# Two blocks' denominators per step, output pairs of a block side by side, and a new order of steps in a gated pair of linear-attention blocks

## The chip, the cores and the metric

One of the eight cores of a Trainium2 chip runs the whole kernel. The metric is the device time of one execution in microseconds (us); lower is better. All times below are in us unless marked ns.

## What is computed

The input x has 2048 tokens of 640 numbers in bf16. Two linear-attention blocks, A and B, read the same x with weights of their own; their outputs are mixed token by token with a gate. Cut to what matters:

```python
def block(x, wqkv, wo):                       # 32 heads of 20 columns
    q, k, v = (x @ wqkv) split in three, each [32, 2048, 20]
    phi = lambda t: where(t > 0, t + 1, exp(t)) + 1e-6
    pq, pk = phi(q), phi(k)
    kv  = einsum("sd,se->de", pk, v)          # per head
    z   = sum over tokens of pk
    num = pq @ kv
    den = pq . z + 1e-6
    return concat_heads(num / den) @ wo

g = sigmoid((x * gate_w).sum(-1))
out = g * block_A(x) + (1 - g) * block_B(x)
```

## The kernel before

The kernel is one core's program whose order is made when it is built. Every instruction is given to a small planner (`Sched`) with its engine, a cost and the buffers that it reads and writes. The planner goes through time by its own costs and fixes the order on each engine and the slot of each pooled buffer; semaphores are then set where one engine depends on another. TensorE alone is different: its steps run in the order written, and that order is the string `MAIN` (L47 to L54). Pools stand for space: `ps` are the 8 banks of PSUM, `eq` three pairs of buffers for exp(q), `po` saved partial sums of the output, `os` and `ot` staging for the output, `gt` and `sv` partial sums of the earlier stages.

The stages, in order of time:

- **K** (to 48 us): x @ Wk for 16 token tiles of 128 and both blocks (L618, L619), then phi on ScalarE and VectorE.
- **G** (`g_unit`, tokens `Gu.n`, L1000): instead of k^T v the kernel forms G = pk^T x for the ten groups of 128 columns of A and B, two groups per unit u = 0 to 4. Each unit is a 2x2 block product done with seven products and sums of operands (Strassen's scheme in Winograd's form), so n runs over 1, 2, 5, 6, 3, 7, 4; a product is eight matmuls of 320 columns, about 1.09 us. Results go through `GT` (L1034, L1105) and a transposing DMA into `GSA` and `GSB`. Extra columns give z, spread by heads into `DEN` (L1048).
- **Q** (`qu_unit`, tokens `Qg.n`, L887): q of the first 1024 tokens (blocks 0 and 1 of 512 tokens), five units of seven products with two or three matmuls of 512 columns. Sums are made on VectorE (`qcm`, L901), then exp and relu on ScalarE (L917, L918), a clip (`qt`, L926) and an add (`qs`, L928) on VectorE give pq.
- **R** (`qp_unit`, tokens `RgX`, L970): q of the other 1024 tokens (blocks 2 and 3) as plain products, ten matmuls of 512 columns into a pair of banks, then exp (L981), relu (L982), clip (L984) and add (L985), each on 1024 columns at once.
- **kvA, kvB** (L1146): kv = G^T Wv per block, masked to the heads on VectorE (`kvm`, L1124). **wA0 to wB1** (`wp_burst`, L1177): kv @ wo in halves, copied out by ScalarE (L1193), written to DRAM (`wpsA`, `wpsB`) and read back as `WP` with another layout. **T1**: four sums of WP's quarters (`t_mat`, L1323).
- **den b** (`den`, L1253): the denominators of block b. Twenty matmuls with 32 columns of weights each: four strips (A and B, two halves of the block) of 256 columns in one bank, five groups of heads summed. VectorE adds the epsilon and multiplies by the gate's factor (L1266; the factor 1 + exp(-+a) was spread by GpSimd at L823 and transposed by a DMA into `GTX`); ScalarE takes ln and exp(-ln) (L1276, L1277). Four DMAs then spread the result over the 128 partitions (`fx`; they read as XN<-PKS for even blocks and TX<-PKS for odd ones), and VectorE scales pq by it (`pqs`, L1309), in two halves for the blocks in `PQH`, block 0 alone.
- **S b** (`s_blk`, L1343): four sums of block b's scaled pq.
- **O** (`Pair`, tokens `Oi.n`, L1378): the output of 256 tokens (pair i = 0 to 7, two per block) as a 2x2 block product with seven products of five matmuls of 320 columns, 0.68 us each, of pq by WP or sums of both. Between them stand copies PSUM to PSUM (o1f, L1417), saves (o2s, o5s, L1394), evictions (o11, o21, L1422, L1443) on ScalarE and sums (o12, o22, L1401) on VectorE. The result is stored in rows of 128 tokens (`o_store`, L1360).

SP issues nearly all DMAs, in the planner's order; ScalarE's queue takes some of wpsB and one of the last stores. SP waits in order, so an issue whose data is late holds all later ones. What sets the order around the change are thus four things: `MAIN` for TensorE, the planner's order on VectorE and ScalarE (an instruction that waits holds all behind it), SP's order, and the bank pairs and `eq` slots that a step must take over from an earlier one.

Of the kernel before, what the change touches and what calls it, by code (L numbers as in the profile page):

```python
# [7 lines left out]
ALU = mybir.AluOpType  # L8
# [3 lines left out]
D = 640  # L12
# [34 lines left out]
MAIN = """G0.1 G1.1 G2.1 G0.2 G1.2 G2.2 G0.6 G0.5 G1.5 G1.6 G1.3 G0.7 G1.7 G0.3 G2.5 G0.4 G1.4 G2.6 Q0.1 G2.3  # L47
Q0.5 Q1.1 Q0.2 Q0.6 Q1.6 Q2.1 Q1.2 Q0.7 Q1.5 Q0.3 Q0.4 Q1.7 G2.7 G3.1 Q3.1 Q2.6 G2.4 Q1.4 Q2.2 Q3.6
Q3.2 G3.2 Q1.3 Q2.5 G4.1 Q3.5 Q2.7 G3.5 Q2.3 Q3.7 Q4.1 G3.6 Q2.4 G3.3 Q3.3 Q4.6 G3.7 Q4.5 Q4.7 Q3.4
G3.4 Q4.3 G4.6 Q4.4 G4.5 Q4.2 kvA G4.2 G4.7 wA0 G4.3 G4.4 wA1 LA den0 R0A kvB den1 wB0 R1A  # L50
S0 R1B R4A R0B wB1 R3A T1 O0.5 O1.5 R2A R3B R2B O0.1 S1 O1.1 R4B O0.2 O1.2 O0.6 O1.6
O1.3 O2.5 den2 O0.7 O3.1 O2.1 O0.3 O3.2 O2.2 O3.5 den3 S2 O0.4 O3.6 O3.3 O1.7 O4.1 O2.6 S3 O4.5
O3.7 O4.6 O2.3 O2.7 O4.2 O5.1 O4.7 O5.5 O5.2 O5.6 O1.4 O4.4 O3.4 O6.1 O6.5 O4.3 O5.7 O6.2 O7.1 O7.5
O2.4 O5.4 O6.6 O5.3 O6.3 O7.6 O7.2 O6.7 O7.7 O7.3 O6.4 O7.4"""  # L54
PB = {}
PQH = (0,)
# [41 lines left out]
class Sched:  # L98
# [97 lines left out]
    def pick(self, b, t, skip=()):  # L196
# [15 lines left out]
        c = [(max(have[i] for i in range(s, s + b.n)), s) for s in b.at if all(i in have for i in range(s, s + b.n))]  # L212
        return min(c) if c else None
# [82 lines left out]
def body(nc, A_x, A_wqkv, A_wo, B_x, B_wqkv, B_wo, gate_w, out, log=None):  # L296
# [79 lines left out]
    OST = {"os": [PKS[:, 8192 + D * k : 8832 + D * k] for k in range(NOS)], "ot": [PKS[:, SSB + D * k : SSB + D * k + D] for k in range(NOT)]}  # L376
# [3 lines left out]
    DNR = PKS[:, SSB + 12288 : SSB + 12800].bitcast(f32)  # L380
    FR = [PKS[:, SSB + 12800 + 256 * n : SSB + 13056 + 256 * n] for n in range(2)]
# [15 lines left out]
    POS = [EKT[:, 644 * k : 644 * k + 640] for k in range(4)] + [PKS[:, 12288 + 640 * k : 12928 + 640 * k] for k in range(5)]  # L397
    POS = [a.bitcast(f32) for a in POS]

# [31 lines left out]
    def dve1(n):  # L431
        return 155 + 1.04 * n
# [383 lines left out]
    dst = GGX.rearrange("p (b k s h) -> p k b s h", b=NB, k=2, s=4)  # L816
    for i, X in enumerate(XS):
        src = (GI if i else GE)[:, :].rearrange("p (b s k) -> p k b s", b=NB, k=2)
        for k in range(2):
            a = src[:, k].unsqueeze(3).to_broadcast([128, NB, 2, 32])  # L820
            op(
                "POOL",
                lambda e, d=dst[:, k, :, 2 * i : 2 * i + 2, :], a=a: e.tensor_scalar(d, a, 1.0, None, op0=ALU.add),  # L823
                600.0,
                ins=bge + [bgi],
                outs=[bx],
                name="ggx",
            )
# [412 lines left out]
    pqs_op, stt_op = {}, {}  # L1241
    bfx = {}

    fx_op = {}

    def den(b):
        ps, b1, b2 = Buf("dn", "ps"), Buf("dr"), Buf("ff")

        def fn(e):
            for g in range(NC):  # L1250
                for s in range(4):
                    i, h = s // 2, s % 2
                    r = e.matmul(  # L1253
                        PS[32 * s : 32 * s + 32, ps.slot, 0:256],
                        ZM[:, NC * i + g, :],
                        PQ[XS[i], b][:, g, 256 * h : 256 * h + 256],
# [5 lines left out]
        op("PE", fn, 850.0, ins=list(bz.values()) + [bpq[b, k] for k in range(2 * NC)], outs=[ps], name="den%d" % b)  # L1262
        ff, gt = FR[b % 2], GTX[:, 256 * b : 256 * b + 256]
        stt_op[b] = op(
            "DVE",
            lambda e: e.scalar_tensor_tensor(DNR, PS[:, ps.slot, 0:256], EPS, gt, op0=ALU.add, op1=ALU.mult),  # L1266
            dve1(256),
            ins=[ps, bgt],
            outs=[b1],
            after=list(stt_op.values()),  # L1270
            prio=-1,
            name="dg%d" % b,
        )

        b3 = Buf("ln")
        op("ACT", lambda e: e.activation(DNR, DNR, ACT.Ln), act_cost(256), ins=[b1], outs=[b3], prio=-1, name="ln%d" % b)  # L1276
        stt_op[b, 1] = op("ACT", lambda e: e.activation(ff, DNR, ACT.Exp, scale=-1.0), act_cost(256), ins=[b3], outs=[b2], after=fx_op.get(b - 2, []), prio=-1, name="rc%d" % b)  # L1277
        fx_op[b] = []
        for i, X in enumerate(XS):
            pqs_op[X, b] = []  # L1280
            hs = []
            for h in range(2):
                src = ff[64 * i + 32 * h : 64 * i + 32 * h + 32, :]
                bx = Buf("fx")
                hs.append(bx)
                fx = FX[X, b][:, 256 * h : 256 * h + 256]
                fx_op[b].append(
                    dma(
                        "SP",
                        "fx%s%d%d" % (X, b, h),  # L1290
                        fx,
                        bass.AP(tensor=src.tensor, offset=src.offset, ap=[src.ap[0], [0, 4], src.ap[1]]),
                        65536,
                        ins=[b2],
                        outs=[bx],
                        after=pqs_op.get((X, b - 2), []),
                        prio=-1,
                        issue=450.0,
                        rate=150.0,
                    )  # L1300
                )
            for lo, hi in ((0, 256), (256, 512)) if b in PQH else ((0, 512),):
                bs = Buf("pqs")
                for h in range(lo // 256, hi // 256):
                    bfx[X, b, h] = bs
# [224 lines left out]
```

## Time and profile before

| what | us |
|---|---|
| median of 3 runs (177.5 to 178.05) | 177.81 |
| the profiled execution | 177.45 |
| its span, first to last instruction | 176.0 |
| TensorE busy in it | 172.0 |
| VectorE busy | 123.6 |
| ScalarE busy | 120.2 |
| granted TensorE clock | 1.0 |

Where TensorE's time goes, by the chain that ended last (shares of the span): O steps 22%, G 21%, K 19% and 6%, R 12%, Q 11%, all others 1% or less each. Times of day in the profiled execution, counted from the span's start: the first G at 48, the first Q at 67.9, kvA at 101.5, den0 at 108.3, kvB at 111.3, the first O at 125.6, den2 at 141.1, den3 at 146.6, the last O ends near 173.8, the last copy at 174.4, and the last store lands at 176.0.

A row of the timeline gives the start, the duration, the engine, the line, the operation, what is written and read and how many; in square brackets how long the engine was idle before it and what ended that. ScalarE's and VectorE's instructions overlap a little when they stand back to back, so starts can be closer than durations. A row of a stretch gives its length, then the busy time of PE, PEld (weight loads), DVE (VectorE), ACT (ScalarE) and POOL (GpSimd), the granted clock, the busy time of the DMA engines and GB/s.

### The profile page before, as it was taken

How to read it: one execution, taken by the hardware profiler on the slowest of the kernel's cores; microseconds unless marked ns; L12 is line 12 of the kernel's file. 1: busy time of each engine (PE TensorE's matmuls, PEld its weight loads, DVE VectorE, ACT ScalarE, POOL GpSimd, SP SyncE). 2: the span in 40 equal slices, each digit the busy share in tenths (PEclk: the TensorE clock that was granted, in tenths of full speed). 3: DMA queues.
4: the chain of work that ended last, by engine and by line, in shares of the span. 5: the costliest groups of instructions: out<-in, count | busy, mean ns of one | idle time of the engine just before them, and what ended most of it. 6: DMA issues, size and time to landing. Idle time of an engine off the chain costs nothing.

```text
span 176.0 us, 3334 instructions
## 1 busy us (share of the span) xinstructions
PE 172.0 (98%) x1323; PEld 108.4 (62%) x1337; DVE 123.6 (70%) x212; ACT 120.2 (68%) x224; POOL 4.9 (3%) x16
## 2 busy tenths in 40 slices
PE   9999999999999999999999999899999999999995
PEld 5555555555577776566666666555555666777773
DVE  2275986999999449574659763469999936995222
ACT  5278888988831214999698938799989745436431
POOL 1000000000002500000000000000000000000000
DMA  7979999300000158982701532877522013413143
GB/s 196 296 142 191 185 375 366 123 2 0 4 0 0 32 101 215 155 124 51 182 0 37 148 79 49 214 158 242 160 49 79 0 56 82 130 47 111 38 149 112
DMA packets 33036, 20.59 MB, mean 117 GB/s; under 512 B 18261, under 2 KB 32893, under 8 KB 33021
## 3 DMA queue, kind: packets, MB, share of 16 engines
q1 hardware_dynamic: 32062, 19.76, 45.1%
q10 hardware_dynamic: 958, 0.63, 1.3%
q8 instruction: 10, 0.16, 0.4%
q14 instruction: 6, 0.04, 0.1%
HBM read 10.88 MB, written 4.26 MB: 86 GB/s over the span
## 4 chain that ended last, share of the span: by engine, by line
PE 96%; ACT 1%; issue 1%; DVE 1%
PE ps L1378 22%; PE ps L1000 21%; PE ps L618 19%; PE ps L970 12%; PE ps L887 11%; PE ps L619 6%; PE ps L547 1%; PE ps L1177 1%; PE ps L1253 1%; PE ps L560 1%; PE ps L1146 1%; ACT EQ L981 1%; ACT EQ L917 0%; DVE PKS L1124 0%; ACT PQ L918 0%
## 5 line engine op out<-in xcount | busy, mean ns | idle before, releaser
L618 PE MATMUL ps<-WKW,XT 128*128 128x512 bf16 x154 | 43.4, 383 | 0.0
L619 PE MATMUL ps<-WKW,XT 128*128 128x128 bf16 (+1 forms) x160 | 35.3, 221 | 0.3
L618 PEld LDWEIGHTS ps<-WKW,XT 128*128 128x128 bf16 x160 | 15.8, 99 | 19.1 <-DVE XT L577 0.3
L664 ACT ACTIVATE EKT<-ps 128x640 bf16<-128x640 f32 x32 | 22.3, 704 | 6.6 <-PE ps L619 5.9
L1000 PE MATMUL ps<-TX,PKS 128*128 128x321 bf16 (+1 forms) x160 | 24.2, 300 | 0.0
L1000 PEld LDWEIGHTS ps<-TX,PKS 128*128 128x128 bf16 x160 | 15.6, 98 | 7.5
L1000 PE MATMUL ps<-XN,PKS 128*128 128x321 bf16 (+1 forms) x120 | 18.0, 300 | 0.0
L619 PEld LDWEIGHTS ps<-WKW,XT 128*128 128x128 bf16 x160 | 15.8, 99 | 0.0
L1029 ACT ACTIVATE EKT<-ps 128x321 f32<-128x321 f32 (+1 forms) x15 | 6.4, 442 | 13.4 <-PE ps L1000 10.9
L1000 PEld LDWEIGHTS ps<-XN,PKS 128*128 128x128 bf16 x120 | 11.5, 98 | 5.3 <-issue 0.2
L744 DVE TENSOR_TENSOR PKS<-PKS 128x1280 bf16<-128x1280 bf16 (+2 forms) x20 | 13.6, 702 | 0.1
L667 DVE TENSOR_SCALAR EKT<-EKT 128x1280 bf16<-128x1280 bf16 (+1 forms) x18 | 8.1, 453 | 5.9 <-ACT EKT L664 5.7
L1034 DVE TENSOR_TENSOR WKW<-ps,EKT 128x320 bf16<-128x320 f32 x15 | 7.3, 489 | 6.9 <-PE ps L1000 6.8
L1401 DVE TENSOR_TENSOR PKS<-ps,PKS 128x320 bf16<-128x320 f32 x11 | 5.4, 489 | 9.0 <-PE ps L1378 8.8
L981 ACT ACTIVATE EQ<-ps 128x1024 bf16<-128x1024 f32 x10 | 10.2, 1022 | 2.0 <-PE ps L970 1.2
L970 PE MATMUL ps<-XT,WQA 128*128 128x512 bf16 x47 | 11.0, 379 | 0.5 <-issue 0.5
L970 PE MATMUL ps<-XT,WQB 128*128 128x512 bf16 x49 | 11.2, 379 | 0.1
L703 DVE SCALAR_TENSOR_TENSOR PKS<-ps,EKT 128x640 bf16<-128x640 f32 x12 | 9.8, 819 | 0.1
L917 ACT ACTIVATE EQ<-ps 128x512 bf16<-128x512 f32 x15 | 9.3, 617 | 1.0 <-DVE ps L901 0.5
L970 PEld LDWEIGHTS ps<-XT,WQB 128*128 128x128 bf16 x50 | 5.9, 117 | 4.8
L970 PEld LDWEIGHTS ps<-XT,WQA 128*128 128x128 bf16 x50 | 5.6, 119 | 4.8 <-issue 0.6
L676 ACT ACTIVATE PKS<-ps 128x640 bf16<-128x640 f32 x12 | 8.4, 698 | 0.0
(141 smaller groups left out, 301.5 us busy)
## 6 DMA issues: line engine op xcount, KB each, us to landing
out_dram<-PKS SPq DMA_DIRECT2D x15, 160.0 KB, 1.8
XN<-in_A_x_dram SPq DMA_DIRECT2D x1, 2240.0 KB, 9.4
WKW<-in_A_wqkv_dram SPq DMA_DIRECT2D x5, 160.0 KB, 3.6
WKW<-in_B_wqkv_dram SPq DMA_DIRECT2D x5, 160.0 KB, 4.0
WQA<-in_A_wqkv_dram SPq DMA_DIRECT2D x1, 800.0 KB, 11.0
WQB<-in_B_wqkv_dram SPq DMA_DIRECT2D x1, 800.0 KB, 13.7
WVA<-in_A_wqkv_dram SPq DMA_DIRECT2D x1, 800.0 KB, 5.0
PKS<-in_B_wqkv_dram SPq DMA_DIRECT2D x1, 800.0 KB, 5.0
```

The source lines that it names most:

```text
L618: e.matmul(a[:, 0:512], l, WK[X][:, c, 0:512], start=(c == 0), stop=(c == NC - 1))
L619: return e.matmul(a[:, 512:w], l, WK[X][:, c, 512:w], start=(c == 0), stop=(c == NC - 1))
L664: op("ACT", lambda e, i=i, ps=ps: e.activation(evg(i), psg(ps), ACT.Exp), act_cost(D), ins=[ps] + first, outs=[ek, b], name="ke")
L676: op("ACT", lambda e, X=X, ps=ps: e.activation(pkt(X, t), psg(ps), ACT.Relu), act_cost(D), ins=[ps], outs=[rk], name="kr")
L703: lambda e, X=X, i=i, ps=ps: e.scalar_tensor_tensor(pkt(X, t), psg(ps), 0.0, evg(i), op0=ALU.max, op1=ALU.add),
L744: lambda e: e.tensor_tensor(out=out, in0=a, in1=b, op=ALU.subtract),
L887: r = e.matmul(PS[:, ps.slot, :], w, x, start=(first and i == 0), stop=(i == len(prs) - 1), skip_group_check=not first)
L917: op("ACT", lambda e: e.activation(EQ[:, eq.slot + h, :], pv(), ACT.Exp), act_cost(512), ins=ins, outs=[eq], name="qe"),
L970: r = e.matmul(PS[:, ps.slot + h, :], WQ[X][:, c, g::5], XT[:, c, 1024 + 512 * h : 1536 + 512 * h], start=(c == 0), stop=(c == NC - 1))
L981: op("ACT", lambda e: e.activation(ev(), pv(), ACT.Exp), act_cost(1024), ins=[ps], outs=[eq], name="qe"),
L1000: r = e.matmul(PS[:, ps.slot, 0:w], reg[:, j, :], mov(j, w), start=(first and j == 0), stop=(j == 7), skip_group_check=not first)
L1378: r = e.matmul(PS[:, ps.slot, 0:HALF], reg(g), mov(g), start=(first and g == 0), stop=(g == NC - 1), skip_group_check=not first)
```

## The change

Seven edits, one diff:

1. `den` takes two blocks (p = 0 for blocks 0 and 1, p = 1 for 2 and 3). Its four strips are A and B of two blocks, 512 columns each; the sum, ln and exp work on 512 columns; a spread is one DMA of 128 KB per block and operand for two of 64 KB. `PQH` is gone: every pqs is one instruction on 2560 columns.
2. The gate's factor is laid out for it: eight GpSimd operations for four, each on half as many columns.
3. Pairs of the blocks in `LOCK` (0, 1, 2) become one object for both halves of a block: a step is two groups of five matmuls into two neighbouring banks, then one copy or sum over both, and stores take two tiles of 128 tokens at once. Block 3 keeps its two pairs.
4. `pick` can take neighbouring slots with conditions on the banks' use.
5. Output staging and saved sums are laid out so that neighbours can be taken together.
6. A store of the upper rows may go out with whichever of its two halves is ready last (`store_a`).
7. `MAIN` is new: kvA stands in the middle of the Q steps, kvB behind the first R, nine of ten R ahead of the first O, den1 behind O0.7, and the G and Q steps are interleaved otherwise.

```diff
-MAIN = """G0.1 G1.1 G2.1 G0.2 G1.2 G2.2 G0.6 G0.5 G1.5 G1.6 G1.3 G0.7 G1.7 G0.3 G2.5 G0.4 G1.4 G2.6 Q0.1 G2.3
-Q0.5 Q1.1 Q0.2 Q0.6 Q1.6 Q2.1 Q1.2 Q0.7 Q1.5 Q0.3 Q0.4 Q1.7 G2.7 G3.1 Q3.1 Q2.6 G2.4 Q1.4 Q2.2 Q3.6
...
-G3.4 Q4.3 G4.6 Q4.4 G4.5 Q4.2 kvA G4.2 G4.7 wA0 G4.3 G4.4 wA1 LA den0 R0A kvB den1 wB0 R1A
-S0 R1B R4A R0B wB1 R3A T1 O0.5 O1.5 R2A R3B R2B O0.1 S1 O1.1 R4B O0.2 O1.2 O0.6 O1.6
-O1.3 O2.5 den2 O0.7 O3.1 O2.1 O0.3 O3.2 O2.2 O3.5 den3 S2 O0.4 O3.6 O3.3 O1.7 O4.1 O2.6 S3 O4.5
...
+MAIN = """G0.1 G1.1 G2.1 G1.2 G2.2 G0.5 G0.2 G0.6 G1.6 G0.7 G0.3 G1.5 G1.7 G2.5 G0.4 G1.3 G1.4 Q1.1 G2.6 Q0.1
+G2.3 Q0.5 Q0.6 Q0.2 Q1.5 Q1.6 Q0.3 G2.7 Q1.2 G3.1 Q2.1 Q1.7 Q3.1 G2.4 Q1.4 Q2.2 Q1.3 G3.2 Q2.6 Q3.2
+G3.5 kvA Q0.7 G4.1 Q2.5 Q0.4 Q2.7 Q3.6 G4.6 Q2.3 Q2.4 Q4.1 G3.6 G3.3 Q3.5 Q4.5 Q3.7 G3.7 Q4.2 Q4.6
+Q4.3 G4.5 Q3.4 Q4.7 G3.4 Q4.4 Q3.3 G4.7 G4.2 wA0 G4.3 G4.4 wA1 den0 R0B kvB R1B S0 wB0 R4A
+R0A R1A R4B wB1 LA T1 R3A R2A R3B S1 O0.5 O0.1 R2B O0.6 O0.2 O0.7 den1 O2.5 O0.3 S2
+O2.1 O0.4 O2.6 S3 O2.2 O2.7 O2.3 O4.1 O2.4 O4.2 O4.5 O6.1 O6.5 O4.6 O6.6 O7.5 O4.3 O4.7 O6.7 O7.1
+O6.3 O6.2 O7.6 O4.4 O7.7 O6.4 O7.3 O7.2 O7.4"""
-PQH = (0,)
+LOCK = (0, 1, 2)
...
-    dst = GGX.rearrange("p (b k s h) -> p k b s h", b=NB, k=2, s=4)
+    dst = GGX.rearrange("p (q k s h) -> p k q s h", q=2, k=4, s=4)
...
-        for k in range(2):
-            a = src[:, k].unsqueeze(3).to_broadcast([128, NB, 2, 32])
+        for k in range(4):
+            a = src[:, k].unsqueeze(3).to_broadcast([128, 2, 2, 32])
...
-    def den(b):
+    def den(p):
...
-                        PS[32 * s : 32 * s + 32, ps.slot, 0:256],
+                        PS[32 * s : 32 * s + 32, ps.slot, :],
                         ZM[:, NC * i + g, :],
-                        PQ[XS[i], b][:, g, 256 * h : 256 * h + 256],
+                        PQ[XS[i], 2 * p + h][:, g, :],
...
-            lambda e: e.scalar_tensor_tensor(DNR, PS[:, ps.slot, 0:256], EPS, gt, op0=ALU.add, op1=ALU.mult),
+            lambda e: e.scalar_tensor_tensor(DNR, PS[:, ps.slot, :], EPS, gt, op0=ALU.add, op1=ALU.mult),
...
-                        "fx%s%d%d" % (X, b, h),
-                        fx,
-                        bass.AP(tensor=src.tensor, offset=src.offset, ap=[src.ap[0], [0, 4], src.ap[1]]),
-                        65536,
+                    "fx%s%d" % (X, b),
+                    fx,
+                    bass.AP(tensor=src.tensor, offset=src.offset, ap=[src.ap[0], [0, 4], src.ap[1]]),
+                    131072,
...
     class Pair:
-        def __init__(self, i):
+        def __init__(self, b, rs):
...
+            self.px, self.py, self.pz = [Buf("o", "ps", n, cover=(HALF,) * n, need=k) for k in (0, HALF, 0)]
+            self.t2, self.t5 = [Buf("po", "po", n) for _ in range(2)]
+            self.oa, self.ob = [Buf("os", "os" if b < 2 else "ot", n) for _ in range(2)]
...
+                for k, r in enumerate(self.rs):
+                    for g in range(NC):
+                        x = e.matmul(PS[:, ps.slot + k, 0:HALF], reg(g, r), mov(g), start=(first and g == 0), stop=(g == NC - 1), skip_group_check=not first)
+                return x
...
+        def copy(self, out, src, ins, outs, after, name):
+            return op("ACT", lambda e: e.activation(out(), src(), ACT.Copy), act_cost(HALF * self.n), ins=ins, outs=outs, after=after, name=name)
...
+                lambda e: e.tensor_tensor(out=self.os(os_, HALF), in0=self.ps(ps), in1=self.pos(src), op=ALU.add),
...
+        def store_a(self):
+            if len(self.bufa) == 2:
+                o_store(self.b, 0, self.rs, self.oa, 0, D, self.bufa)
...
-    pairs = [Pair(i) for i in range(8)]
+    pairs = {}
+    for b in range(NB):
+        for rs in ((0, 1),) if b in LOCK else ((0,), (1,)):
+            pairs[2 * b + rs[0]] = Pair(b, rs)
```

## The prediction

> **What bounds the kernel now.** I read the busy table first, then the chain of waits, then the table of who waited for whom.
>
> ```profile
> PE 172.0 (98%) x1323; PEld 108.4 (62%) x1337; DVE 123.6 (70%) x212; ACT 120.2 (68%) x224; POOL 4.9 (3%) x16
> ...
> PE 96%; ACT 1%; issue 1%; DVE 1%
> ...
> PE ps L1177 <- DVE PKS L1124: 0.5, 1, 0.5
> ```
>
> TensorE is on 96% of the chain. The span is 176.0 us and the run took 177.45, so 1.45 lies around the span; the median of the runs is 177.81. TensorE's only wait for another engine of half a microsecond is the last line: wpB0 waits for the masked copy after kvB. So a change can win little: TensorE work that vanishes and that wait. It can lose wherever another engine comes late. Which one is near that is told by the busy time in stretches of 2 us (PE, PEld, DVE, ACT) and the timeline of the stage from den0 on:
>
> ```profile
> 116.00:118.00 2.00, 2.00 (x11) 1.06 (x10) 1.96 (x3) 1.97 (x5) 0.00 (x0) 1.00 0.94 188
> ...
> 120.00:122.00 2.00, 2.00 (x11) 1.10 (x10) 2.00 (x4) 1.78 (x3) 0.00 (x0) 1.00 0.91 286
> ...
> 128.00:130.00 2.00, 2.00 (x11) 1.11 (x10) 2.00 (x5) 2.00 (x4) 0.00 (x0) 1.00 0.25 68
> ```
>
> ```profile
> 112.95 2.67 SPq L417 DMA_DIRECT2D XN<-PKS  x4
> ...
> 116.04 1.56 DVE L1309 TENSOR_TENSOR PQ<-PQ,XN 128x1280 bf16<-128x1280 bf16 x2 [1.49 <-DMA XN<-PKS]
> 116.26 2.32 PE L970 MATMUL ps<-XT,WQB 128*128 128x512 bf16 x10
> ...
> 116.67 1.01 ACT L981 ACTIVATE EQ<-ps 128x1024 bf16<-128x1024 f32 x1
> ...
> 117.57 1.02 ACT L982 ACTIVATE PKS<-ps 128x1024 bf16<-128x1024 f32 x1
> ...
> 124.69 1.49 DVE L1309 TENSOR_TENSOR PQ<-PQ,TX 128x2560 bf16<-128x2560 bf16 x1
> ```
>
> From 116 to 140 TensorE, VectorE and ScalarE are all full. VectorE enters this stage only when the spread 1/denominator (fx) has landed at 116.04: it sat idle 1.49 for it. From then on it has no slack; an engine that is not on the chain decides here.
>
> **The change part by part.**
>
> *Denominators.* A den of 256 columns takes 0.66 (108.26 to the next weight load at 108.92); its five groups of four strips are 0.107 apart. With 512 columns each group is 0.107 longer: 0.66 + 5 x 0.107 = 1.19. Four at 0.66 become two at 1.19: 2.64 - 2.38 = **-0.26**. Behind them the sum on 512 columns takes 0.69 (as L901) for 0.42, and ln and exp about 0.60 (as L917) for 0.42: fx is ready some 0.6 later, near 111.6. That is covered: SP is issuing the five stores of wpsA until 112.91 and reaches fx at 112.95 in both. The cover gone, it would cost 0.6.
>
> *wpB0.* den1 (0.66) lay between kvB and wpB0, now R1B (2.16, from 116.26 to the next ten at 118.42). The masked copy needs 0.69 and two hops: **-0.47** (112.34 + 0.66 = 113.00 against 113.53, less a usual gap).
>
> *The order from den0 on.* Nine of the ten R units, kvB, wpB0 and wpB1 now stand ahead of the first O step. The built program's order on VectorE, from the landing L of the first fx on: pqsA0, pqsB0, a clip (qt), pqsA1, pqsB1, S1 of block 0, and only then the qs of R1B, which frees the exp buffer for R1A. pqs starts are 1.40 apart (124.69 to 126.09), a qt takes 0.33 and an S 0.74 start to start, a qs 0.69: that qs ends at L + 0.05 + 4 x 1.40 + 0.33 + 0.74 + 0.69 = L + 7.41. ScalarE then does R1A's exp (start to start 0.91) and relu (1.02), with 0.12 for hops: L + 9.46. R3A needs R1A's banks. TensorE is there at 108.26 + 1.19 (den0) + 6 x 2.157 (R) + 1.06 (kvB) + 2 x 0.54 (wp) + 0.43 (gaps as before) = 124.96. So TensorE waits L - 115.5. Before, the same lateness was there and cost nothing: RB0's exp ran at 125.70, 3 us behind its product's end at 122.74, but wpB1, R3A and two O5 in other banks stood behind it on TensorE.
>
> L: the same place before was 112.95 + 3.1 = 116.05 for 64 KB, of which half a block; now the first piece is 128 KB. The second 64 KB costs, at the 284 GB/s that 112 to 114 moved, 0.23. L = 116.3, the wait **+0.8**. Bounds for L from the rows of this same transfer: 112.95 + 2.3 = 115.25 (the quiet set at 143) and 112.95 + 4.9 = 117.85 (the set issued at 117.8, amid wpsB):
>
> ```profile
> XN<-PKS SPq DMA_DIRECT2D x1, 64.0 KB, 3.1
> ...
> TX<-PKS SPq DMA_DIRECT2D x4, 64.0 KB, 4.9
> ...
> XN<-PKS SPq DMA_DIRECT2D x4, 64.0 KB, 2.3
> ```
>
> I take the first, nearest in place and traffic. (The Trainium skill, "DMA: Bandwidth & Descriptors", section on the anatomy of one DMA, fits a transfer by 2.0 us plus its bytes over 436 GB/s; for another issuing path than this one. By it 128 KB land after 2.3 us, L is 115.25 and no wait arises; the row at this place, 3.1 for half the bytes, speaks against it.)
>
> A second wait follows. ScalarE next hangs on R4A's qs: after R1B's qs VectorE does T1 (0.90), a qt, three S, a qt and this qs, 4.4 together: L + 11.8. From there ScalarE does four R units' exp and relu (8 x 0.91), waits some 0.4 for two more qs, then the copies o5s and o1f (0.6 + 0.7) and hops: L + 21 = 137.3. O0.6 needs o1f and would be reached at 108.26 + 27.62 of work + 0.45 of gaps + 0.8 = 137.13: **+0.2**.
>
> *Pairs in lockstep.* The same 56 groups of five matmuls; 28 pairs of copies become joint ones for blocks 0 to 2. A 640-wide copy takes 0.70 (row of L664) for two of 0.44, a 640-wide sum 0.82 (L703) for two of 0.49. So each engine works less, and one result comes 0.26 to 0.33 later. Cover: between a product and its user stands another step of 1.36 or an R of 2.16, against 0.2 + 0.70. Followed from O0.6 to the end with these rows I find no wait: den1 at 141.5 needs the last qs at 140.4, O4.1 at 153.7 needs pqsA2 at about 150, O4.5 at 157.8 needs S1 of block 2 at 156.3. Cost 0; without cover up to 0.9 a step. Stores: 17 become 11; the last are again 160 KB, then two of 80 KB on two queues, so the tail of about 2.2 stays. Store out310 hands its slot on from out300, issued four steps earlier: 1.8 to land against 3.5 of steps.
>
> *Gate spread (L823).* Four GpSimd operations of 256 become eight of 128: 3.66 us (2.00 + 1.66) becomes between 3.66 and 7.3. A 20-element memset takes 0.125, so most of 0.9 scales: 8 x 0.51 = 4.1 taken. The reciprocal ahead of it comes 0.4 sooner. The transposing DMA behind it, then gsA0 in SP's queue, then c22 and P4 of unit 1 have 1.0 us of slack: cost 0, at the far end 1.6.
>
> *G and Q order, kvA early.* kvA moves from 101.5 to about 83.5. It needs wvA and the last transpose of A, issued near 71; the one before took 8.1 to land, so 79.1: 4.4 to spare. Its two masked copies (0.69) now sit in VectorE's queue ahead of a qcm with 0.6 to spare. ScalarE is the tight one here (2.00 of 2.00 from 72 to 78). I laid the new step order beside it: least slack 0.15, at Q4.4 (qcm of Q4.7) and at wpA1, which now takes both pairs of wpA0's banks: two copies (0.2 + 0.87 + 0.97) against P4.3 and P4.4 (2.18). Cost 0, bounds -0.4 (the gaps of this stage now) to +1.
>
> Sum: -0.26 - 0.47 + 0.8 + 0.2 = **+0.3** (rounded). 177.45 becomes 177.75; the median stands 0.36 above that profile, so **178.1**. Its own range is 177.6 to 178.7.
>
> **The rivals.**
>
> *R1, fx early: faster.* If L is 115.3 or less, no wait arises: -0.73, 177.1. For it: the quiet rows of 2.1 to 2.3. Against: five stores of 700 KB are just ahead, as before, where it took 3.1. The Trainium skill's fit, named above, belongs here: by it the time is 177.1.
>
> *R2, fx late: slower.* Every 0.1 of L above 115.5 is 0.1 of TensorE's time, since VectorE and ScalarE are full until O0.6. As the second set (4.9), L is 117.85: 2.35 + 0.2 - 0.73 = +1.8, 179.6. It decides against the kernel from L = 116.0 on. For it: double pieces, and block 1's share of fx now leaves in the same burst. Against: wpsB is not yet issued at 112.95.
>
> *R3, ScalarE late at wpA1: slower.* The queue behind Q4.4 and Q3.3 holds three exps and three relus, about 3.3 us at 0.5 each with their waits, and ends near 105.0 where wpA0's copies should start at 105.3. Each 0.1 of lateness over 0.2 is 0.1 at wpA1. One late round of exp, relu and sum, 1.2, gives +1.0 on top: 179.1. Against: before, ScalarE was idle 2.8 ahead of these copies.
>
> *R4, strips not side by side:* 20 x 0.216 = 4.3 a den, +6. The rows show four at once; I give it nothing.
>
> **How the numbers follow.** My case 0.46, R1 0.28, R2 0.16, R3 0.10. No change is within 0.3%, 0.53 us, about what a measurement of this kernel can tell. My case ends 0.29 within and 0.17 slower; R1 0.24 faster and 0.04 within; R2 0.16 slower; R3 0.08 slower and 0.02 within. Faster 0.24, the same 0.35, slower 0.41. The range goes from R1 with some of the G and Q stage's gaps gained, 176.9, to R2 with its far bound, 179.8.
>
> **What would show it.** A den near 1.19; no wait of L1177 for the masked copy; TensorE waiting once near 125, at R3A, for ScalarE, and ScalarE before that for VectorE; VectorE's first pqs behind a DMA near 116.3. Wrong if that pqs starts before 115.5 and R3A still waits, if TensorE waits ahead of den0, or if an O step waits after den1.

## The result, and the profile after

The changed kernel takes 178.81 us (median of 13 runs, 178.06 to 179.82); the kernel before, run beside it, 177.50 (13 runs, 177.32 to 178.05). The ratio is 1.0068, its 95% interval 1.0050 to 1.0085: slower by 0.9 to 1.5 us, with a wider spread than before. The forecast was 178.1, with no change and slower as the likeliest outcomes. Some short names stand for much below: fx is the transfer that spreads 1/denominator, L the moment when its first piece has landed, a clip (qt) and an add (qs) finish the q of an R unit on VectorE, and a product (pqs) scales q by fx.

The busy table and the first line of the chain that ended last, of the changed kernel:

```profile
PE 172.6 (97%) x1282; PEld 107.5 (60%) x1297; DVE 121.9 (69%) x202; ACT 118.1 (66%) x205; POOL 6.3 (4%) x20
...
PE 79%; DVE 9%; DMA 4%; POOL 3%; ACT 2%; SPq 1%; issue 1%; DVEq 0%; ACTq 0%
```

VectorE and ScalarE have less to do than before, as the joint copies and sums promised (123.6 to 121.9, 120.2 to 118.1), and the span is 177.8 for 176.0 all the same. TensorE's share of the chain fell from 96% to 79%: work of other engines now lies on it, in two places. The chain itself, in order of time (start, duration, what), shows both:

```profile
56.01 5.04 POOL WKW L828 x8
...
61.06 1.24 SPq L422
...
62.35 2.75 DMA GSA<-WKW
...
109.24 1.22 PE ps L1256 x20
...
113.85 3.94 DMA XN<-PKS
...
117.81 1.49 DVE PQ L1302
119.31 1.40 DVE PKS L1302
...
124.58 0.61 DVE XT L990
...
125.28 1.02 ACT EQ L986
126.31 0.92 ACT PKS L987
...
127.27 2.79 PE ps L975 x12
```

The first place is the gate spread on GpSimd (L828), with two transfers behind it. The second is fx (XN<-PKS), which lands at 117.8, then VectorE's queue up to the qs of R1B (L990), then ScalarE's exp and relu of R1A (L986, L987), then R3A. The table of waits has one long entry for TensorE:

```profile
PE ps L975 <- ACT PKS L987: 1.4, 1, 1.4
```

and the busy time in stretches of 2 us has VectorE nearly idle at 116 (DVE 0.18; 1.96 before) and TensorE short of work at 126 (PE 0.73; 2.00 before). First the changed kernel:

```profile
116.00:118.00 2.00, 2.00 (x23) 1.18 (x23) 0.18 (x1) 1.84 (x3) 0.00 (x0) 1.00 0.33 64
126.00:128.00 2.00, 0.73 (x4) 0.44 (x5) 2.00 (x5) 2.00 (x4) 0.00 (x0) 1.00 0.33 86
```

and the second stretch in the kernel before:

```profile
126.00:128.00 2.00, 2.00 (x14) 1.26 (x13) 2.00 (x3) 1.92 (x3) 0.00 (x0) 1.00 0.69 186
```

How far each place reaches is read from the start times of TensorE's own steps. From the first G (L1000 before, L1005 after) to the first product of den0 it takes 60.32 before and 60.83 after: 0.5 lost. From den0's first product to wpB1's end it takes 16.71, with nothing lost, and R3A then waits 1.39. The first G itself starts anywhere from 47.7 to 48.6 in the profiles of all kernels here; that is no part of the change.

### The profile page after: what moved, and what is told of

Its sections match the earlier page's. It is cut to its first block, busy times and chain, and to the rows that moved or that the text cites. A ratio compares the mean times of both kernels' runs of the same rounds, so it can differ in the third digit from the quotient of the medians.

```text
span 177.8 us, 3198 instructions
## 1 busy us (share of the span) xinstructions
PE 172.6 (97%) x1282; PEld 107.5 (60%) x1297; DVE 121.9 (69%) x202; ACT 118.1 (66%) x205; POOL 6.3 (4%) x20
## 4 chain that ended last, share of the span: by engine, by line
PE 79%; DVE 9%; DMA 4%; POOL 3%; ACT 2%; SPq 1%; issue 1%; DVEq 0%; ACTq 0%
PE ps L1373 22%; PE ps L623 19%; PE ps L1005 13%; PE ps L892 10%; PE ps L624 6%; PE ps L975 5%; POOL WKW L828 3%; DMA XN<-PKS 2%; DVE PQ L1302 2%; DVE PKS L1302 2%; DMA GSA<-WKW 2%; PE ps L552 1%; SPq L422 1%; PE ps L1256 1%; DVE WKW L845 1%
## 5 line engine op out<-in xcount | busy, mean ns | idle before, releaser
L1005 PE MATMUL ps<-TX,PKS 128*128 128x321 bf16 (+1 forms) x160 | 24.6, 300 | 0.1
L1005 PEld LDWEIGHTS ps<-TX,PKS 128*128 128x128 bf16 x160 | 15.5, 98 | 8.1 <-DVE DEN L1053 0.3
L1005 PE MATMUL ps<-XN,PKS 128*128 128x321 bf16 (+1 forms) x120 | 18.2, 300 | 0.0
L1005 PEld LDWEIGHTS ps<-XN,PKS 128*128 128x128 bf16 x120 | 11.6, 98 | 5.4 <-issue 0.2
L986 ACT ACTIVATE EQ<-ps 128x1024 bf16<-128x1024 f32 x10 | 10.2, 1026 | 4.5 <-PE ps L975 1.7
L1397 ACT ACTIVATE PKS<-ps 128x640 bf16<-128x640 f32 (+2 forms) x14 | 7.7, 552 | 7.2 <-PE ps L1373 7.2
L1039 DVE TENSOR_TENSOR WKW<-ps,EKT 128x320 bf16<-128x320 f32 x15 | 7.3, 488 | 6.5 <-DMA GSA<-WKW 3.8
L1412 DVE TENSOR_TENSOR PKS<-ps,EKT 128x640 bf16<-128x640 f32 x6 | 4.9, 822 | 6.8 <-PE ps L1373 6.8
L1397 ACT ACTIVATE ps<-ps 128x640 f32<-128x640 f32 (+1 forms) x5 | 3.0, 596 | 8.6 <-PE ps L1373 8.6
```

The lines of the kernel that those rows point to most:

```text
L986: op("ACT", lambda e: e.activation(ev(), pv(), ACT.Exp), act_cost(1024), ins=[ps], outs=[eq], name="qe"),
L1005: r = e.matmul(PS[:, ps.slot, 0:w], reg[:, j, :], mov(j, w), start=(first and j == 0), stop=(j == 7), skip_group_check=not first)
L1397: return op("ACT", lambda e: e.activation(out(), src(), ACT.Copy), act_cost(HALF * self.n), ins=ins, outs=outs, after=after, name=name)
```

## The experiments

Times are medians. The kernel before was run beside each group of kernels, on the same chip (177.56 to 177.67), and ratios stand against that. "Changed kernel" is the one predicted. Differences between kernels are differences of medians; what the ratios make of them stands beside where it is another number. In the expectations T1, T1b and T2 are theories: T1, that R3A waits because fx is late and six operations stand on VectorE between its landing and the qs of R1B; T1b, that the sum of VectorE's and ScalarE's work binds whatever its order; T2, that the eight small GpSimd operations hand over late. The step T1 of `MAIN` is another thing and is called "the step T1" here. Where an expectation writes O6.0, O5.0 and the like, it names `MAIN`'s O0.6, O0.5, with the product first. c22 is VectorE's sum at L1039 that waits for gsA0, the first transposed piece of GSA, and P4 of unit 1 is G1.4.

**spread4: the eight small GpSimd operations back to four.**

```diff
-        src = (GI if i else GE)[:, :].rearrange("p (q s k) -> p k q s", q=2, k=4)
-        for k in range(4):
-            a = src[:, k].unsqueeze(3).to_broadcast([128, 2, 2, 32])
+        src = (GI if i else GE)[:, :].rearrange("p (q s k) -> p q k s", q=2, k=4)
+        for q in range(2):
+            a = src[:, q].unsqueeze(3).to_broadcast([128, 4, 2, 32])
```

> The changed kernel, but the gate spread on GpSimd (L823 to L828) is again four operations of 256 elements where the change makes eight of 128; the order of every other engine is that of the changed kernel. T2 (the eight small operations hand gtx, gsA0 and with them P4 of unit 1 over late): the spread takes 3.7 us where it took 5.06, the transposing DMA is issued near 59.8 instead of 61.06, c22's wait for gsA0 (3.83 on VectorE) shrinks, the 0.32 wait of P4 and most of the issue gaps behind it are gone, first G to den0 is 60.3 instead of 60.9 and the time falls by 0.4 to 0.6 us. Rival (the 0.58 is lost by the new order of G, Q and kvA): the time stays within 0.2 us of the changed kernel's. In both, the wait at R3A near 125 stays about 1.4.

Measured: 178.29 us (177.92 to 178.74, 12 runs), ratio 1.0034 [1.0023, 1.0046], against 1.0068 for the changed kernel. The groups on GpSimd (line, engine, shapes, count, then busy time and mean ns of one), first of the changed kernel:

```profile
L828 POOL TENSOR_SCALAR WKW<-GE 128x128 bf16<-128x128 f32 x4 | 3.0, 784 | 54.9 <-DVE GI L819 54.9
L828 POOL TENSOR_SCALAR WKW<-GI 128x128 bf16<-128x128 f32 x4 | 2.0, 525 | 0.0
```

and of spread4:

```profile
L828 POOL TENSOR_SCALAR WKW<-GE 128x256 bf16<-128x256 f32 x2 | 2.2, 1104 | 54.8 <-DVE GI L819 54.8
L828 POOL TENSOR_SCALAR WKW<-GI 128x256 bf16<-128x256 f32 x2 | 1.7, 844 | 0.0
```

By the second row of each pair, an operation on half the elements takes 0.525 for 0.844, more than half; the whole spread takes 5.06 for 3.8. With four operations the transposing DMA behind it starts at 59.70 instead of 61.06, and first G to den0 is 60.34. Eight kernels here with four operations and the new step order show 60.34, three with eight show 60.83, and the kernel before, profiled twice, 60.32 and 60.33. So T2 holds, the loss is 0.5 in the trace, and the new order of G, Q and kvA costs nothing. The wait at R3A is unchanged (1.4).

**pqs_late: block 1's products later on VectorE, by a due time.**

```diff
-PB = {}
+PB = {1: 200000}
```

> The changed kernel, but VectorE takes block 1's two products with fx (L1302) and its sums only after the qs of the R units, by a later due time (PB); the orders of TensorE and SyncE are unchanged. T1 (R3A waits because fx is late and VectorE's queue has six operations between the landing and the qs that R1A's exp waits for): with 2 x 1.40 and a sum of 0.74 out of that chain the qs of R1B comes some 2.8 earlier, the 1.4 wait at R3A is gone, and the time falls by 1.0 to 1.4 us, unless block 1's products are then late for O2.5. Rival (VectorE and ScalarE are full from 116 to 140, so their sum of work binds and not its order): the wait moves to another R or O step and at least 1.0 of the 1.4 stays.

Measured: 178.81 us (177.99 to 179.23, 6 runs), ratio 1.0058 [1.0036, 1.0080]; the wait at R3A is 1.4 as before. That is no verdict on theory T1: the edit did not move the qs. The planner put two more sums of block 0 where it had taken one product away, and the qs of R1B starts at 124.06, 6.76 behind the first product; in the changed kernel it is 124.50 and 6.69. A due time fixed what came later, not what came in its place.

**both: the two edits together.**

> The two edits together: four gate operations, and block 1's products behind the qs on VectorE. T1 and T2: the gains add, 1.4 to 2.0 us under the changed kernel, 176.8 to 177.4 us, at or under the kernel before. Rivals: only one of the two gains, or neither.

Measured: 178.16 us (177.67 to 178.97, 12 runs), ratio 1.0028 [1.0012, 1.0044]: spread4's gain, and none from the due time, with the R3A wait at 1.3.

**fx_act: fx issued from ScalarE's queue.**

```diff
                 dma(
-                    "SP",
+                    "SP" if p else "ACT",
                     "fx%s%d" % (X, b),
```

> The changed kernel, but the four fx transfers of blocks 0 and 1 are issued from ScalarE's queue, right behind the exp that makes them, where the change has them on SyncE behind the five stores of wpsA. T1 with the cause of the late fx in SyncE's queue: fx is ready at 112.5 and was issued at 113.85, so the first product of VectorE starts up to 1.3 earlier, near 116.5, and the wait at R3A falls from 1.4 to 0.1 to 0.4; the time falls by about 1.0 us. Rival a (the transfers share the engines with wpsA wherever they are issued): landing takes longer by what the issue is earlier, no change. Rival b (VectorE and ScalarE bind by their sum of work): fx is early and the wait moves.

Measured: 179.34 us (179.04 to 179.71, 6 runs), ratio 1.0092 [1.0075, 1.0109]: no gain, and by the medians 0.5 worse, though this interval overlaps with that of the changed kernel. ScalarE's timeline in this kernel (start, duration; "ACTq" is its issuing, and in brackets the idle time before an operation):

```profile
112.56 1.39 ACTq L422 DMA_DIRECT2D XN<-PKS  x2
113.98 2.38 ACTq L422 DMA_DIRECT2D TX<-PKS  x2
116.40 1.02 ACT L986 ACTIVATE EQ<-ps 128x1024 bf16<-128x1024 f32 x1 [3.87 <-PE ps L975]
```

Four issues held ScalarE for 3.87, and TensorE then waited 1.8 at R4A. The issue came 1.3 earlier than in the changed kernel, and fx was there hardly earlier. The DMA view has the first piece alone (its size, then us from issue to landing):

```profile
XN<-PKS ACTq DMA_DIRECT2D x1, 128.0 KB, 5.1
```

From 112.56 that is 117.7, where the changed kernel has 117.8. VectorE's first product started at 117.80, right behind a clip, so it does not show the landing itself. ScalarE's queue is not slow as such: in this kernel 112.5 KB of wpsB took 2.7 to land from it and 3.1 from SyncE. This speaks for rival a: an fx issued while the stores of wpsA go out landed late, although it left from another queue. (The Trainium skill says in "DMA: Bandwidth & Descriptors", issuing engines are not separate DMA queues: transfers issued from different engines run on the same 16 DMA engines. This trace agrees: 1.3 earlier out, 0.1 earlier in.)

**qs1_first: one qs moved.** On spread4; VectorE's order from den0 on, the rest unchanged (qt is L989, qs L990, pqs L1302, S L1336; B1 stands for R1B):

```diff
-qtB0 qsB0 pqsA0 pqsB0 qtB1 pqsA1 pqsB1 S1_0 qsB1 T1 qtA4 ...
+qtB0 qsB0 pqsA0 pqsB0 qtB1 qsB1 pqsA1 pqsB1 S1_0 T1 qtA4 ...
```

> The kernel of spread4 with one operation of VectorE moved: the qs of R1B (L990) stands ahead of block 1's two products with fx and of S1 of block 0; the orders of all other engines, and the rest of VectorE's, are unchanged. T1 (the place of that one qs behind the late fx makes R3A wait): the qs starts near 120.3 instead of 123.9, R1A's exp follows its product, the 1.4 wait at R3A is gone and the time falls by 1.2 to 1.4 us, to about 177.0. T1b (VectorE and ScalarE are full between the landing of fx and O6, so their sum binds): the wait at R3A goes, but R4B's exp still waits for the qs of R4A, which has not moved, the same 1.2 to 1.4 come back by O6.0, and the time stays within 0.2 us of spread4's.

Measured: 178.06 us (177.54 to 178.49, 12 runs), ratio 1.0025 [1.0012, 1.0038]: 0.2 under spread4, where theory T1 wanted 1.2 to 1.4. ScalarE and TensorE in this kernel:

```profile
128.06 1.02 ACT L986 ACTIVATE EQ<-ps 128x1024 bf16<-128x1024 f32 x1 [1.43 <-DVE PKS L990]
...
137.23 1.52 PE L1373 MATMUL ps<-GSB,XN 128*128 128x320 bf16 x10 [0.77 <-ACT ps L1397]
```

R3A no longer waits, but R4B's exp waits 1.43 for the next qs, that of R4A, which had not moved; ScalarE stays late up to o1f, and O0.6 (the second line) waits for that. The stall went on by one link. Theory T1 as I had put it, one operation in the wrong place, falls.

**qs_all: the whole of VectorE's order anew.** On spread4, no work added or left out; on ScalarE one relu and one exp change places:

```diff
-qtB0 qsB0 pqsA0 pqsB0 qtB1 pqsA1 pqsB1 S1_0 qsB1 T1 qtA4 S1_1 S2_0 S3_0 qtA0 qsA4 qtA1 S2_1 ...
+qtB0 qsB0 qtB1 pqsA0 pqsB0 qsB1 qtA4 S1_0 qsA4 qtA0 S2_0 qsA0 qtA1 T1 qsA1 S3_0 S4_0 pqsA1 ...
```

> The kernel of spread4 with VectorE's whole order from den0 on written anew: every qs (L990) stands as soon as its relu is done, block 1's products and sums behind them; on ScalarE one relu and one exp change places. No work is added or left out. T1: no R step waits, ScalarE no longer idles for a qs (1.5, 0.65 and 0.3 in the changed kernel), O6.0 comes 1.3 to 1.5 earlier and the time falls by 1.2 to 1.5 us against spread4, to 176.8 to 177.1. T1b: with fx landing where it does, the sum of VectorE's and ScalarE's work up to O6 binds whatever the order, and no more than 0.4 is gained. Risk in both: T1's load of wpsA has not landed where T1 now stands, or an S of block 1 is late for O5 of that block.

Measured: 177.10 us (176.62 to 177.51, 12 runs), ratio 0.9976 [0.9962, 0.9989]: 1.2 under spread4 (1.0 by the ratios), and faster than the kernel before. R1A's exp and R3A in this kernel:

```profile
123.22 1.07 ACT L986 ACTIVATE EQ<-ps 128x1024 bf16<-128x1024 f32 x1
...
125.57 4.51 PE L975 MATMUL ps<-XT,WQA 128*128 128x512 bf16 x20
```

Neither has an idle time before it. The first product with fx starts at 117.31, 8.39 behind den0's first product (8.64 in the changed kernel), and fx itself landed in this profile 3.4 after its issue at 113.60, that is 8.1 behind. At one for one, as the prediction has it, the old order would still have waited 0.8 to 1.1 for that. T1b falls as well: the same work in another order fits.

**fx_first: fx ahead of three stores on SyncE.** On spread4; all other orders unchanged:

```diff
-wpsA000 wpsA001 wpsA010 wpsA011 wpsA012 fxA0 fxB0 fxA1 fxB1 wplA0
+wpsA000 wpsA001 fxA0 fxB0 wpsA010 wpsA011 wpsA012 fxA1 fxB1 wplA0
```

> The kernel of spread4 with one change of order on SyncE: fx of block 0 (A and B) is issued ahead of the three stores of wpsA out of WVA instead of behind them; the orders of all other engines are unchanged. If fx is late because the stores of wpsA are ahead of it on the DMA engines (fx_act issued it 1.3 earlier, and it landed at nearly the same moment): it is issued as soon as the exp that makes it is done, VectorE's first product starts 1.3 to 2.0 earlier, the wait at R3A is 0 to 0.2 and the time falls by 1.0 to 1.4 us. T1b has the same here, since VectorE begins its full stretch earlier. Rival (128 KB from 32 partitions to 128 takes 3.9 whatever is ahead of it): only the 1.3 of the issue is won, and the wait at R3A stays at 0.1 to 0.3. Risk: wpsA lands later, and T1, which stands right behind the qs of R1B on VectorE, waits for it and holds the next qs back.

Measured: 177.03 us (176.44 to 177.49, 12 runs), ratio 0.9967 [0.9953, 0.9981]: 1.3 under spread4 (1.2 by the ratios) and 0.5 under the kernel before. SyncE, VectorE and TensorE:

```profile
112.00 1.30 SPq L422 DMA_DIRECT2D XN<-PKS  x2
...
115.48 1.49 DVE L1302 TENSOR_TENSOR PQ<-PQ,XN 128x2560 bf16<-128x2560 bf16 x1 [0.45 <-DMA XN<-PKS]
...
125.30 4.51 PE L975 MATMUL ps<-XT,WQA 128*128 128x512 bf16 x20
```

The first product starts 6.84 behind den0's (8.64 in the changed kernel). VectorE's order, six operations between landing and qs, is the old one and costs nothing now. Of these 1.8 the issue makes 1.3 (3.36 behind den0 for 4.68) and the landing, 3.48 for 3.96, the rest. Only the first part is sure: with the same order on SyncE fx took 4.0 to land in fx_qs and 3.66 in fx_unlock. In fx_act it left at this same moment, 3.36 behind den0, but amid the three stores, and took 5.1. The step T1, which I feared for, did not wait in this profile.

**den_only: the new denominators with the old step order.** Two dens of 512 columns, pairs one by one, four gate operations; the lines show `MAIN` of the kernel before and of this one:

```diff
-... R0A kvB den1 wB0 R1A ... O2.5 den2 O0.7 ... O3.5 den3 S2 O0.4 ...
+... R0A kvB R1A wB0 ... O2.5 den1 O0.7 ... O3.5 S2 O0.4 ...
```

> One part alone: the new denominators (two of 512 columns) with the kernel before's step order, pairs one by one and four gate operations; den1 is taken out from between kvB and wpB0 and R1A moved there, and den2 becomes den1. If the joint denominators by themselves bring the late fx: fx of the first two blocks is issued and lands as in the changed kernel (about 4 after its issue), VectorE enters its full stretch 1.3 later than in the kernel before, TensorE waits at an R or an O5 step for 0.5 to 1.5, and the time is 177.5 to 178.5 against 177.67 for the kernel before. If the new order of the steps from den0 on makes it: no wait above 0.3, and the time is 176.9 to 177.3, by 0.26 + 0.47 under the kernel before.

Measured: 184.19 us (182.94 to 185.18, 6 runs), ratio 1.0364 [1.0327, 1.0402]; the two expectations missed by 5.7 and 6.9. An R step waits 0.5, but the loss is further on, where neither expectation had it: O4.5 waits 3.9 for a sum of block 2 (L1337 in this kernel). den1 now needs every R unit and serves blocks 2 and 3 at once, so block 2's fx is issued at 145.27 (143.21 before), and VectorE takes block 3's two products ahead of block 2's sums. The old order asks for block 2 before it is there. In the changed kernel, whose O steps take blocks 0 and 1 through first, the waits show no O step that waits for a sum. So the new order of the O steps is a need of the joint denominators, as far as these two kernels tell; whether another order on VectorE alone would do was not tried.

**fx_qs: both remedies.** The orders of fx_first and qs_all together, on spread4.

> The edits of fx_first and qs_all together on spread4: fx of block 0 ahead of three of wpsA's stores, and every qs ahead of block 1's products and sums. Theory now held (one stall, made by a late fx times six operations between it and the qs that frees ScalarE's exp buffer; either remedy alone takes the whole of it): TensorE already waits for nobody in either of the two, so the gains do not add and the time is that of fx_first and qs_all, 176.9 to 177.1; with slack left on both sides the runs may lie closer together. Rival (each took away a part, and the throughput of VectorE and ScalarE still costs something): a further 0.3 to 0.8 less, 176.3 to 176.7.

Measured: 177.06 us (176.66 to 177.54, 12 runs), ratio 0.9977 [0.9965, 0.9989]. The gains do not add: it is one stall, and either remedy takes the whole of it.

**fx_unlock: fx_first without the lockstep.** The joint pairs of blocks 0 to 2 taken apart, step by step:

```diff
-LOCK = (0, 1, 2)
+LOCK = ()
-... O0.5 O0.1 R2B O0.6 O0.2 ...
+... O0.5 O1.5 O0.1 O1.1 R2B O0.6 O1.6 O0.2 O1.2 ...
```

> The kernel of fx_first with the lockstep undone: each step of the joint pairs of blocks 0 to 2 becomes two steps of five products, one right behind the other, with copies, sums and stores of one half each, as in the kernel before; the orders up to O5.0 are unchanged. The prediction took the lockstep at 0: the time is fx_first's within 0.2 us, no O step waits in either. Rival a (the joint copies pay, because ScalarE or VectorE is near the bound in the O stage): without them an O step waits and the time is 0.3 to 1.0 more. Rival b (a joint result that comes 0.26 to 0.33 later costs): 0.3 to 0.9 less.

Measured: 177.38 us (176.57 to 178.31, 12 runs), ratio 0.9989 [0.9972, 1.0006], where fx_first has 0.9967 [0.9953, 0.9981]. The medians favour the lockstep by 0.35, though the intervals overlap. TensorE's longest wait, then two lines of VectorE and ScalarE that lead up to it:

```profile
PE ps L1374 <- ACT ps L1398: 0.6, 1, 0.6
...
123.79 0.99 DVE L1317 TENSOR_TENSOR GSB<-PKS 128x1600 bf16<-128x1600 bf16 x1 [1.21 <-DMA PKS<-wpsA]
...
128.29 1.02 ACT L987 ACTIVATE EQ<-ps 128x1024 bf16<-128x1024 f32 x1 [1.50 <-DVE PKS L991]
```

That is O0.6 waiting for o1f. It looks like rival a, but the trace says otherwise. The four single copies take ScalarE from 135.97 to 137.44, 1.47; fx_first's two joint ones take from 135.05 to 136.39, 1.34, which is only 0.13 less. What is late is the step T1: the load of wpsA took 6.4 to land (5.2 in fx_first), the step T1 waited 1.21 for it, the qs behind it and R4B's exp came late, and ScalarE was 1.4 late before the first copy. The edit touches neither the stores of wpsA nor that load, so this wait says little of the lockstep. Later one more O step waits 0.2 for a sum. What the lockstep is worth stays open, between nothing and some 0.4.

**fx_half: the first piece of fx in halves.** On spread4, behind all the stores, product in halves too:

```diff
+                for lo in (0, 256) if (X, b) == ("A", 0) else (0,):
+                    n = 256 if (X, b) == ("A", 0) else 512
...
-                    131072,
+                        256 * n,
```

> The kernel of spread4 with fx of block 0, A, in two pieces of 64 KB and its product with fx (L1302) in two halves of 1280 elements, as the kernel before has them; it stays behind wpsA's stores, and all orders stay. If the size of the piece makes the landing (3.1 for 64 KB in the kernel before, 3.8 to 4.0 for 128 KB): VectorE starts 0.7 to 0.9 earlier after the issue, the wait at R3A falls from 1.4 to 0.5 to 0.8 and the time by 0.3 to 0.8 us against spread4. If the traffic of wpsA ahead makes it: the first half lands 3.5 to 4.0 after its issue and nothing is gained; the extra issue makes fx B later by 0.6 at most, covered by the first product.

Measured: 178.88 us (178.03 to 179.62, 6 runs), ratio 1.0071 [1.0045, 1.0097]; nothing gained, and by the medians 0.6 over spread4. VectorE's timeline:

```profile
116.86 1.56 DVE L1305 TENSOR_TENSOR PQ<-PQ,XN 128x1280 bf16<-128x1280 bf16 x2 [2.00 <-DMA XN<-PKS]
...
125.02 0.99 DVE L1319 TENSOR_TENSOR GSB<-PKS 128x1600 bf16<-128x1600 bf16 x1 [0.72 <-DMA PKS<-wpsA]
```

The 64 KB, issued at 113.16, took 3.70; that is 8.38 behind den0 against 8.71 in spread4, and R3A waited 1.1 for 1.4. What was won there was lost again: the load of wpsA took 7.7 to land (5.4 in spread4) and came late for the step T1 (second line, 0.72), so R2B and O0.6 waited too. Whether the one issue more on SyncE made it late, one trace doesn't tell.

**before_again: the kernel before, profiled once more.**

> The kernel before, unchanged, for a second look at one transfer: the prediction priced the landing of fx by 3.1 (64 KB, issued at 112.95, one profile), and kernels with the same five stores of wpsA ahead of it have since shown 3.3 to 4.0 for 128 KB and 3.7 for 64 KB. If the piece's size makes the landing: 3.0 to 3.2 again. If it is the traffic ahead, which varies from run to run: anything from 3.0 to 4.0, and the time does not follow it, since nothing on TensorE's chain waits for it here.

Measured: 177.92 us (one run; 177.89 beside it). Issue 113.42, first half product 116.51: 3.09 once more. So this does not say that the quick landing of the kernel before was chance. Behind the same stores, 64 KB took 3.09 twice there but 3.70 in fx_half, and 128 KB took 3.31 (den_only), 3.4 (qs_all), 3.43 (qs1_first), 3.83 (both), 3.94 (pqs_late), 3.96 (changed) and 4.02 (spread4). What spreads these was not settled, and neither was whether the size of the piece or the traffic makes them. What the runs do show is what the place of the issue does: fx ahead of three of the stores had landed 6.8 to 7.4 behind den0 (fx_first, fx_unlock, fx_qs), and fx issued as early but amid them 8.5 (fx_act).

## Why the prediction was right or wrong

*The forecast as a whole.* 178.1 was 0.7 short; the measured 178.81 lies within the range and outside my case's own 177.6 to 178.7. Slower, the likeliest of the three, came true. As a change the forecast was further off. It added 0.3 to a median of 177.81 from three runs, while the kernel before took 177.50 beside the changed one: the change is 1.3, and that the base was 0.3 too high hid a part of the error by luck. Two terms of the sum were too small, and together they make up the missing 1.0: the gate spread's by 0.5 and the wait's at R3A by 0.6. The first of them is also one of the prediction's own signs of being wrong, time lost on TensorE ahead of den0.

*Denominators, -0.26, and wpB0, -0.47: right, as far as seen.* A den takes 1.22 and 1.19, for 1.19. TensorE no longer waits at wpB0. With both losses taken out (fx_first) the rest of the change comes to a ratio of 0.9967, that is 0.6 us faster, 0.3 to 0.8 by the interval; the two terms say 0.73. That the two terms alone make it was not tried: the one kernel with the denominators by themselves, den_only, loses elsewhere.

*The wait at R3A: mechanism right, size wrong.* The prediction had the chain operation by operation: landing, five products and sums with the clip between, qs of R1B, exp and relu of R1A, R3A. From the landing to R3A it gave 9.46; the trace has 127.27 - 117.81 = 9.46. From den0 to TensorE's arrival it gave 16.70; the trace has 16.71. All of the error is in L, which the prediction put 8.04 behind den0 and the trace 8.64. The issue of fx is where it was forecast, 4.68 behind den0 for 4.69, so the term that was too small is the landing: 3.1 for 64 KB and 0.23, from a stretch's bandwidth, for the second 64 KB. It took 3.96 in this profile, and 3.31 to 4.02 in the seven kernels that have 128 KB at this place. Whether it was the 0.23 or the 3.1 that failed is open, since 64 KB took 3.70 in fx_half. (The five stores ahead are 225, 150, 225, 150 and 50 KB, 800 together and not the 700 of the prediction.) L is 116.9 by the prediction's clock, within its bounds and on the far side of R2's 116.0: what happened stands between my case and R2, with R2's price of 0.1 for every 0.1; fx_half bears the price out, 8.38 and a wait of 1.13 against 8.64 and 1.39. The runs of this kernel spread by 1.8 us and those of the kernel before by 0.7. That a transfer has come onto TensorE's chain would fit, but spread4 has the same wait and its runs spread by 0.8 only, so the cause of the wider spread is open. (The Trainium skill's fit in "DMA: Bandwidth & Descriptors", anatomy of one DMA, given there for another issuing path, makes an estimated 2.3 us for this transfer; no landing of it behind these stores was under 3.3, and the measurement decides.)

*What the wait is made of* took the experiments. The prediction called VectorE and ScalarE full until O0.6 and made every 0.1 of L a 0.1 of TensorE's time. That holds for the order in the kernel only. qs_all leaves fx behind the stores and loses nothing; fx_first leaves the order and loses nothing. The stall needs two things at once, a late fx, and products and sums of work not yet due in front of each qs, and it is enough to remove either. For ScalarE "full" was too strong already: its stretches from 130 and from 136 in the kernel before have 1.32 and 1.40 of 2.00.

*The second wait, 0.2 at O0.6:* 0.1 in the trace (R2B ends at 138.66, O0.6 starts at 138.77). With one qs moved, and no wait at R3A, it was 0.77; the two waits are one lateness, taken at one place or the other.

*The gate spread, cost 0: wrong, by its own rule.* The kernel before has these two rows (busy time and mean ns behind the bar):

```profile
L823 POOL TENSOR_SCALAR WKW<-GE 128x256 bf16<-128x256 f32 x2 | 2.0, 1012 | 55.0 <-DVE GI L814 55.0
L823 POOL TENSOR_SCALAR WKW<-GI 128x256 bf16<-128x256 f32 x2 | 1.7, 842 | 0.0
```

"8 x 0.51 = 4.1 taken": the second four took 0.525 each, as taken; the first four 0.784 each, and why these are dearer is open. So 5.06, 1.40 more than before; over the slack of 1.0 that the prediction gave, 0.4 is left, and 0.5 was measured. The slack was right, the price was taken near the cheap end of 3.66 to 7.3 by the row of a memset, which is another operation, and the far end's 1.6 was left out of the rivals.

*Pairs in lockstep, 0:* in the changed kernel no O step but O0.6 waited for a joint result, and that for 0.1. Undoing the lockstep moved the median by 0.35 with intervals that overlap, and the wait seen there has another cause, so 0 is neither shown nor refuted. *G and Q order, 0, and R3:* right, 60.34 against 60.32 and 60.33 from the first G to den0 with four operations. *R4:* no, a den takes 1.2.

## What to carry to other kernels

Where a result frees a buffer for another engine, let that operation stand ahead of work that nobody waits for yet, through the whole stage: moving one such operation only hands the stall to the next (0.2 won of 1.4 here), moving all of them won 1.0 to 1.2. A transfer whose result starts a full stage goes out ahead of stores that nobody waits for yet: a change of place in one queue was worth 1.2 to 1.3 here, while another issuing queue or smaller pieces were worth nothing. The same goes for an operation that waits for a load and stands in front of one that frees a buffer: the load of wpsA took 4.4 to 7.7 to land here, and in two kernels the step T1 waited for it and passed the wait on. Splitting an operation of 0.84 on GpSimd gave two of 0.525, so count it as more time, and look what hangs behind it.

## What the runs showed of the hardware that was not expected

In den_only TensorE stood idle from 151.7 to 155.66, and the stretches after it (TensorE's granted clock is the third value from the end) ran at half the clock or near it:

```profile
154.00:156.00 2.00, 0.34 (x2) 0.23 (x3) 2.00 (x3) 0.00 (x0) 0.00 (x0) 0.68 0.00 0
156.00:158.00 2.00, 2.00 (x9) 1.12 (x8) 1.81 (x3) 0.44 (x1) 0.00 (x0) 0.50 0.00 0
158.00:160.00 2.00, 2.00 (x9) 1.16 (x8) 1.22 (x2) 0.12 (x1) 0.00 (x0) 0.50 0.00 0
```

The clock was 0.62 from 160 to 162 and 1.00 from 162 on: a wait of 3.9 cost another 2.8 (2 x 0.50 + 2 x 0.50 + 2 x 0.38). With the 0.5 of the R step that is 7.2, the 183.2 of this profile against the 176.0 of the kernel before; the 0.73 that the new denominators and wpB0 should have won is then still to be found. The wait of 1.4 at R3A cost nothing of the kind: twenty products right behind it took 4.51, as in qs_all. (The Trainium skill, "TensorE: Matmul & The Clock Gate", Part 1, has the clock halved after an idle window of about 3.4 us; both waits agree with it, though here the clock fell somewhat sooner. The stretches of 1 us have 0.85 from 154 to 155 and 0.50 from 155 on, so by them it fell near 154.7, about 3.0 after the last product, and the measurement decides.) And in fx_act four issues of 128 KB took ScalarE 3.87 us, nearly 1 us each, in which it computed nothing.
